# Attention and feed-forward on one core: another formula for the small part of the exponential, and one product for the linear path

## The chip, the cores and the metric

One of the eight cores of one Trainium2 chip runs the whole program. The metric is the time that the device needs for one execution, in microseconds; every time below is one of those or comes from one profiled execution. The engines are named as the profile names them: PE (TensorE's matmuls; PEld its weight loads), DVE (VectorE), ACT (ScalarE), POOL (GpSimd) and SP (SyncE, which here only issues DMAs).

## The reference

Shapes: `q` is 4 x 12288 x 128, `kv` 4 x 384 x 32 x 128, `w_sr` 128 x 128, `w_in` 128 x 2048, `w_out` 2048 x 128.

```python
kv_pool = kv.reshape(B, H // 4, 4, W // 4, 4, C).mean(axis=(2, 4))   # 768 keys per batch
k = v = kv_pool.reshape(B, -1, C) @ w_sr
s = (q @ k.transpose(0, 2, 1)) / np.sqrt(C)
a = np.exp(s - s.max(-1, keepdims=True))
x = (a / (a.sum(-1, keepdims=True) + 1e-09)) @ v                     # 49152 tokens x 128
h = x @ w_in
out = (h - np.tanh(h)) @ w_out
```

## The kernel before

The scores are small (the keys are taken about their mean), so exp(s) is split into 1 + s and a small rest exp(s)-1-s. The part 1 + s needs no scores at all: its product with the values is the 128 x 128 matrix M (the sum over keys of value times key) applied to q. Only the rest goes through the 768 keys. In the same way h - tanh(h) is taken about the batch's mean token: a first-order part, which is the 128 x 128 matrix A applied to the token's difference from the mean, and a third-order part, which needs the 2048 hidden values and is computed as h²(h+1) after a scaling.

Tokens are worked on in 96 groups of 512 (24 per batch). What one group needs, with the names and lines of the code:

- `rounded_q` (ACT, L1095) rounds q to the type that PE takes at its full rate (fp32r), and `lower_q` (POOL, L1148) keeps what the rounding lost.
- `scores` (PE, L1111): three tiles of 128 x 1024, each from two matmuls, in PSUM tiles called `big`, of which there are three. `exps` (ACT, L1115) takes exp, `beyond` (DVE, L1118) makes exp(s)-1-s in f16 (the tiles `r2`).
- The three `r2` tiles are summed in memory by DMAs: `copied` (SP) copies the first, `added` (POOL's queue, L1134) adds the second and the third. `shares` (PE, L1139) sums over the keys, and `share_left` (ACT, L1158) makes from it the factor t of every token.
- `straight` (PE, L1144) is M times q in three matmuls: upper part of M times rounded q, lower part of M times rounded q, upper part of M times the rest of q. `values` (PE, L1154) adds six matmuls of the values with `r2` into the same PSUM bank. `apart` (DVE, L1165) multiplies by t and gives df, the token's difference from the mean.
- `rounded` (POOL, L1168) rounds df to dr, and `lower_left` (POOL, L1194) keeps the rest, dl.
- The layer: `forth` (PE, L1225) makes eight `big` tiles of hidden values from dr. In seven of them `square` (ACT, L1229) and `cube` (DVE, L1232) make h²(h+1); in the eighth ACT copies (L1236) and POOL does one addition (L1239) and two products (L1243). `back` (PE, L1264) adds sixteen matmuls of the results into the bank `acc`, and another `straight` (PE, L1214) adds A times df, again in three matmuls. `result` (ACT, L1275) moves `acc` to SBUF and SP stores it.

That is 52 matmuls of 512 columns for each group. All of this overlaps: while a group's layer runs, the scores of groups two and three ahead are made. PSUM has eight banks: three `big` tiles of two banks, one bank `acc`, and one bank called `x`, which the sum over the shares, then the bank of `straight` and `values`, and the small products between batches use in turn.

The order is not written out by hand. Each operation is handed to a `Plan` with a label (`AT[...]` in eighths of a group's time, or an entry of the long list `PLACES`), an engine, a booked duration and the tiles it reads and writes. On each engine the operations of one lane are kept in the order of their labels; a label says which comes first on its own engine and is no time, so labels of two engines are not compared. Engines execute their queues in order, and so do the DMA queues of SP and POOL.

Before a batch starts, its keys are pooled by sixteen accumulating DMAs (L612, in POOL's queue, one per group), M and A are made, the scaled weights `winr` and `Wr` are made on POOL (L983, L1034), and the first-order terms are summed (L860 and L863 on DVE, L876 onwards on POOL, L1014 on POOL). Much of that runs beside the groups of the batch before. Ahead of the first group lie the loads of the weights and keys, and a conversion of the 64-bit words of the weights. At the end a verdict (`fits`) tests whether the approximations hold for the inputs; if they do not, a slow exact version runs afterwards.

Of the kernel before, what the change touches and what calls it, by code (L numbers as in the profile page):

```python
# [35 lines left out]
NEAR = 2.0**-12  # L36
# [7 lines left out]
LARGEST = 30000.0  # L44


class Plan:
# [3 lines left out]
    SOON = 0.1  # L51

# [46 lines left out]
    def run(self, between):  # L99
# [33 lines left out]
        while any(ready.values()):  # L133
            best = None
            for e, q in ready.items():
                if q:
                    starts = []
                    for r, i in q:
                        held = free.get("port", 0.0) if self.ops[i][5] else 0.0
# [13 lines left out]
            if port:  # L153
                free["port"] = now + us
# [35 lines left out]
    "within ym.i.3": -1236.8394829, "add win32 4": -1236.2365152, "first_stat stat": -1236.0688716,  # L190
# [14 lines left out]
    "apart df.3": -903.3427419, "rows norms 2": -903.3316533, "beyond r2.5.1": -903.3302341,  # L205
# [1381 lines left out]
```

## Time and profile before

| what | us |
|---|---|
| median of 3 runs (1278.62 to 1280.59) | 1279.99 |
| the profiled execution: span from the first to the last instruction | 1278.0 |
| PE busy (98% of the span), 5488 matmuls | 1252.7 |
| DVE busy (96%) | 1221.1 |
| ACT busy (93%) | 1188.8 |
| POOL busy (90%) | 1145.4 |

No separate time of the profiled execution is given; the median is 2.0 us above the span, which is what lies around it. Matmuls overlap in the pipeline and their ends are modelled, so PE's busy time says little: how long one holds PE is read from the starts of consecutive ones. The same holds in a smaller measure for the other engines, where an instruction begins before the shown end of the one ahead of it.

### The profile page before, as it was taken

The numbers are of one execution on the slowest core, as the hardware profiler recorded it, in microseconds if no ns is written. First come the engines' busy times: TensorE is split into PE (matmuls) and PEld (weight loads), VectorE is DVE, ScalarE is ACT, GpSimd is POOL, SyncE is SP. The second block draws the span as 40 slices with busy tenths as digits, with TensorE's granted clock in tenths as the row PEclk, the third lists the DMA queues.
The fourth block names the chain that finished last, engine by engine and source line by source line (L and its number), as shares of the span: only waits on it lengthen the run. The fifth ranks groups of instructions, "written<-read, shape, count | busy, mean of one in ns | idle before, by whom it ended". The sixth has DMA issues, their size and how long they took to land.

```text
span 1278.0 us, 17320 instructions
## 1 busy us (share of the span) xinstructions
PE 1252.7 (98%) x5488; PEld 880.8 (69%) x5488; DVE 1221.1 (96%) x1180; ACT 1188.8 (93%) x1416; POOL 1145.4 (90%) x981
## 2 busy tenths in 40 slices
PE   8999999999999999999999999999999999999997
PEld 7766676676767666676766767667667676766765
DVE  5999999999999999999999999999999999999996
ACT  4899999899999999999999999989999999999995
POOL 3799999899999997999999998999898988889886
PEclk9999999999999999999999999999999999999999
DMA  9276667347666653355666664344444444444431
GB/s 361 65 150 144 133 138 149 87 100 154 148 131 141 149 127 102 99 133 118 134 145 131 142 149 112 91 124 103 119 101 108 100 107 114 103 115 99 107 91 34
DMA packets 82947, 158.46 MB, mean 124 GB/s; under 512 B 9920, under 2 KB 12096, under 8 KB 82848
## 3 DMA queue, kind: packets, MB, share of 16 engines
q0 software_dynamic: 33552, 66.99, 31.7%
q1 hardware_dynamic: 49296, 90.29, 20.5%
q8 instruction: 45, 0.74, 0.3%
q14 instruction: 54, 0.44, 0.1%
HBM read 57.93 MB, written 25.39 MB: 65 GB/s over the span
## 4 chain that ended last, share of the span: by engine, by line
PE 70%; POOL 19%; issue 4%; DVE 3%; DMA 2%; ACT 2%; SPq 0%; POOLq 0%; DVEq 0%; ACTq 0%
PE big L1225 21%; PE acc L1264 20%; PE big L1111 9%; PE x L1154 7%; POOL rp L1243 5%; PE x L1144 4%; PE acc L1214 4%; POOL z L1243 4%; PE x L1139 3%; POOL rs L1134 3%; POOL ql L1148 2%; POOL z L1239 2%; POOL dr L1168 2%; DVE r L1118 1%; ACT E L1115 1%
## 5 line engine op out<-in xcount | busy, mean ns | idle before, releaser
L1232 DVE SCALAR_TENSOR_TENSOR r<-big,u 128x1024 fp32r<-128x1024 f32 x672 | 778.1, 1218 | 14.0 <-ACT u L1229 13.7
L1229 ACT ACTIVATE u<-big 128x1024 f32<-128x1024 f32 x672 | 661.8, 1033 | 35.0 <-PE big L1225 22.8
L1225 PE MATMUL big<-dr,winr 128*128 128x512 f32 x1536 | 510.1, 413 | 4.2 <-DVE r L1118 2.6
L1264 PE MATMUL acc<-r,Wr 128*128 128x512 f32 x1344 | 426.7, 410 | 0.6 <-DVE r L1232 0.6
L1118 DVE SCALAR_TENSOR_TENSOR r<-E,big 128x1024 f16<-128x1024 f32 x288 | 350.3, 1218 | 13.9 <-ACT E L1115 8.3
L1225 PEld LDWEIGHTS big<-dr,winr 128*128 128x128 f32 x1536 | 276.4, 188 | 101.0 <-DVE r L1118 26.1
L1115 ACT ACTIVATE E<-big 128x1024 f32<-128x1024 f32 x288 | 295.6, 1028 | 12.3 <-PE big L1111 2.3
L1264 PEld LDWEIGHTS acc<-r,Wr 128*128 128x128 f32 x1344 | 252.2, 188 | 64.6 <-DVE r L1232 1.5
L1243 POOL TENSOR_TENSOR rp<-z,v 128x1024 fp32r<-128x1024 f32 x96 | 258.9, 2697 | 0.2
L1243 POOL TENSOR_TENSOR z<-z,v 128x1024 f32<-128x1024 f32 x96 | 231.9, 2416 | 7.8
L1134 POOL DMA_DIRECT2D rs<-r x188 | 204.4, 1087 | 4.0 <-DMA rs<-r 2.3
L1111 PE MATMUL big<-qr,kTr 128*128 128x512 f32 x576 | 191.6, 414 | 0.4 <-ACT kTr L740 0.4
L1154 PE MATMUL x<-r,vvr 128*128 128x512 f16 x576 | 174.5, 385 | 0.0
L1194 POOL TENSOR_TENSOR dl<-df,dr 128x512 fp32r<-128x512 f32 x96 | 162.7, 1695 | 0.0
L1148 POOL TENSOR_TENSOR ql<-q,qr 128x512 fp32r<-128x512 f32 x96 | 161.4, 1681 | 0.5 <-ACT qr L1095 0.5
L1168 POOL TENSOR_SCALAR dr<-df 128x512 fp32r<-128x512 f32 x96 | 71.4, 744 | 76.0 <-DVE df L1165 72.1
L1111 PEld LDWEIGHTS big<-qr,kTr 128*128 128x128 f32 x576 | 101.3, 188 | 47.6 <-DVE r L1118 26.6
L1239 POOL TENSOR_SCALAR z<-v 128x1024 f32<-128x1024 f32 x96 | 111.4, 1161 | 0.5 <-ACT v L1236 0.5
L1236 ACT COPY v<-big 128x1024 f32<-128x1024 f32 x96 | 97.5, 1016 | 0.8 <-PE big L1225 0.6
L1154 PEld LDWEIGHTS <-vvr 128*128 128x128 f16 x576 | 33.5, 98 | 77.8 <-issue 77.5
L1264 PE MATMUL acc<-rp,Wr 128*128 128x512 f32 x192 | 77.0, 483 | 4.2 <-POOL rp L1243 4.0
L1275 ACT ACTIVATE o<-acc,At 128x512 f32<-128x512 f32 x96 | 65.8, 685 | 10.1 <-PE acc L1264 10.0
(182 smaller groups left out, 992.3 us busy)
## 6 DMA issues: line engine op xcount, KB each, us to landing
rs<-r POOLq DMA_DIRECT2D x188, 256.0 KB, 3.6
q<-in_q_dram SPq DMA_DIRECT2D x96, 256.0 KB
out_dram<-o SPq DMA_DIRECT2D x96, 256.0 KB
rs<-r SPq DMA_DIRECT2D x94, 256.0 KB
kvp<-in_kv_by_place_dram POOLq DMA_DIRECT2D x45, 384.0 KB, 5.2
winr<-in_kv_first_dram SPq DMA_DIRECT2D x8, 384.0 KB
kc<-inverse SPq DMA_DIRECT2D x12, 256.0 KB
r<-in_kv_by_key_dram SPq DMA_DIRECT2D x4, 512.0 KB
```

What stands on the lines that cost most here:

```text
L1111: PE.matmul(out=half(plan[s], h), lhsT=plan[kTr][:, n * P : (n + 1) * P], rhs=plan[qr], start=True, stop=True)
L1115: A.activation(out=plan[e], in_=plan[s], func=AF.Exp)
L1118: V.scalar_tensor_tensor(out=plan[r], in0=plan[e], scalar=-1.0, in1=plan[s], op0=ALU.add, op1=ALU.subtract)
L1134: PL.dma_start(out=plan[rs], in_=plan[r2s[k]], accum_op=ALU.add)
L1148: PL.tensor_tensor(out=plan[ql], in0=plan[qs], in1=plan[qr].bitcast(F32), op=ALU.subtract)
L1154: PE.matmul(out=plan[num], lhsT=plan[vvr][:, n], rhs=half(plan[f"r2.{g}.{k}"], h), start=(start and h == 0), stop=(stop and h == 1))
L1194: PL.tensor_tensor(out=plan[dl], in0=plan[df], in1=plan[dr].bitcast(F32), op=ALU.subtract)
L1225: PE.matmul(out=half(plan[hp], h), lhsT=plan[winr][:, f * P : (f + 1) * P], rhs=plan[dr], start=True, stop=True)
L1229: A.activation(out=plan[u], in_=plan[hp], func=AF.Square)
L1232: V.scalar_tensor_tensor(out=plan[r], in0=plan[hp], scalar=1.0, in1=plan[u], op0=ALU.add, op1=ALU.mult)
L1243: PL.tensor_tensor(out=plan[to], in0=plan[x], in1=plan[y], op=ALU.mult)
L1264: PE.matmul(out=plan[acc], lhsT=plan[Wr][:, 2 * n + h], rhs=half(plan[r], h), start=(start and h == 0), stop=(stop and h == 1))
```

## The change

- exp(s)-1-s becomes 4.5 ln(1-s/3)². ACT takes the logarithm of the score tile and writes w in f16 (128 x 1024); POOL multiplies w by itself (on DVE in the first three groups only). The factor 4.5 goes into the values and into t. DVE no longer reads the scores.
- All eight hidden tiles go through `square` on ACT and `cube` on DVE; the copy, the addition and the two products of the eighth are gone.
- The linear part of the attention passes to the output as one composed matrix B = M·A/K (K = 768): the layer's `straight` is now B upper times qr, B lower times qr, B upper times ql, and A times dl, where dl = df - M·q/K holds the small rest only. In the attention one matmul of M with rounded q stays, and a new DVE operation `keep` copies M·q/K out of the bank before `values` adds to it. B is made once per batch by a matmul (`through`), two ACT operations and a POOL subtraction.
- `share_left` moves from ACT to DVE. The nine products `first_times` of the later batches move from DVE to POOL.
- Buffers: six of `qr` and four of `ql` instead of five and two, six of `r` instead of four and two of `rp`, two of `rs` instead of three; the word tiles of the weights all use the three buffers `u` (one of each four had a tile of its own before).
- New labels in `AT` and a new list `PLACES`; the first five groups have no lanes; the verdict's early part starts fourteen groups before the end instead of twenty-four.

```diff
+            def roots(s=s, w=w):
+                A.activation(out=plan[w], in_=plan[s], func=AF.Ln, scale=-1.0 / 3, bias=1.0)
+            def beyond(w=w, r=r, k=k):
+                (V if k in on_v else PL).tensor_tensor(out=plan[r], in0=plan[w], in1=plan[w], op=ALU.mult)
-            def exps(s=s, e=e):
-                A.activation(out=plan[e], in_=plan[s], func=AF.Exp)
-            def beyond(s=s, e=e, r=r):
-                V.scalar_tensor_tensor(out=plan[r], in0=plan[e], scalar=-1.0, in1=plan[s],
-                                       op0=ALU.add, op1=ALU.subtract)
...
-        def straight(start, stop):
-            upper, lower = (plan[Mh][:, n] for n in range(2))
-            for n, (x, y) in enumerate(((upper, qr), (lower, qr), (upper, ql))):
-                PE.matmul(out=plan[num], lhsT=x, rhs=plan[y], start=(start and n == 0),
-                          stop=(stop and n == 2))
+        def straight():
+            PE.matmul(out=plan[num], lhsT=plan[Mh], rhs=plan[qr], start=True, stop=True)
+        def keep():
...
+                V.tensor_scalar(out=plan[kept], in0=plan[num], scalar1=1.0 / K, scalar2=None, op0=ALU.mult)
...
         def share_left():
...
+                V.tensor_scalar(out=plan[t], in0=plan[den], scalar1=-THIRD_OF / K**2, scalar2=1.0 / K,
+                                op0=ALU.mult, op1=ALU.add)
...
         def lower_left():
-            PL.tensor_tensor(out=plan[dl], in0=plan[df], in1=plan[dr].bitcast(F32), op=ALU.subtract)
+            PL.tensor_tensor(out=plan[dl], in0=plan[df], in1=plan[kept], op=ALU.subtract)
...
-            upper, lower = (plan[Ah][:, n] for n in range(2))
-            for n, (x, y) in enumerate(((upper, dr), (lower, dr), (upper, dl))):
+            upper, lower = (plan[Bh][:, n] for n in range(2))
+            for n, (x, y) in enumerate(((upper, qr), (lower, qr), (upper, ql), (plan[Ah], dl))):
...
-    ON_POOL = (0,)
...
-            V.tensor_tensor(out=plan[f"pr.{b}.{n}"], in0=winT[:, 4 * n : 4 * n + 4], in1=by, op=ALU.mult)
+            PL.tensor_tensor(out=plan[f"pr.{b}.{n}"], in0=winT[:, 4 * n : 4 * n + 4], in1=by, op=ALU.mult)
...
-    WORDS = {"i": ("u", "u", "u", "E"), "o": ("u", "u", "u", "z")}
+    WORDS = {"i": ("u", "u", "u", "u"), "o": ("u", "u", "u", "u")}
...
-        then=[6.19, 2.26, 3.01, 6.54, 1.52, 7.28, 8.03, 0.77],
-        back=[11.04, 6.93, 7.24, 7.85, 6.32, 8.76, 9.37, 5.71],
...
-        copied=-18.59, added=[-15.50, -11.66],
-        shares=-7.54, left=-6.81, straight=-6.02, apart=-2.72, rounded=-2.20, rounded_q=-24.34,
-        slope=4.93, result=11.47, lower_q=-12.50, lower_left=2.65, gather=-6.93)
+        rounded_q=-22.5, scores=[-24.19, -22.96, -21.97], roots=[-19.69, -19.48, -17.1],
+        beyond=[-17.77, -16.37, -16.06], copied=-18.97, added=[-15.26, -9.25], shares=-7.62,
+        left=-7.27, lower_q=2.48, straight=-6.63, keep=-5.82, values=[-4.43, -5.77, -5.74],
+        apart=-4.74, rounded=-1.06, lower_left=3.44,
+        forth=[-1.26, 0.4, 1.08, 1.64, 2.28, 4.6, 4.6, 4.93],
+        first=[2.36, 4.36, 5.05, 6.45, 7.24, 7.44, 8.85, 10.18],
+        then=[0.24, 1.97, 2.9, 3.19, 4.85, 5.21, 6.47, 7.21],
+        back=[4.13, 5.37, 6.96, 8.98, 5.8, 8.25, 9.57, 9.35], slope=4.85, result=14.11,
```

## Rows read from the trace of the kernel before

**Rows 1.** Output copies on ACT: count, shortest/median/longest, first and last start in us.

```profile
L1275 ACT ACTIVATE o<-acc,At x96: 673/686/693, 70.8 to 1271.3; 128x512 f32<-128x512 f32 x96
L1275 ACT ACTIVATE o<-acc,At x9: 677/686/688, 1143.9 to 1241.4; 128x512 f32<-128x512 f32 x9
```

**Rows 2.** PE in order of time: start, length, instruction; xN merges neighbours.

```profile
1110.11 0.63 PE L1225 MATMUL big<-dr,winr 128*128 128x512 f32 x2
1110.58 0.63 PE L1264 MATMUL acc<-r,Wr 128*128 128x512 f32 x2
1111.04 0.62 PE L1225 MATMUL big<-dr,winr 128*128 128x512 f32 x2
```

**Rows 3.** DVE in order of time, one group's work.

```profile
1111.83 8.07 DVE L1232 SCALAR_TENSOR_TENSOR r<-big,u 128x1024 fp32r<-128x1024 f32 x7
1119.82 2.50 DVE L1118 SCALAR_TENSOR_TENSOR r<-E,big 128x1024 f16<-128x1024 f32 x2
1122.24 0.68 DVE L1165 TENSOR_TENSOR df<-x,t 128x512 f32<-128x512 f32 x1
1122.93 1.22 DVE L1118 SCALAR_TENSOR_TENSOR r<-E,big 128x1024 f16<-128x1024 f32 x1
1124.07 1.23 DVE L1232 SCALAR_TENSOR_TENSOR r<-big,u 128x1024 fp32r<-128x1024 f32 x1
```

**Rows 4.** Stretches with a batch change: length, then busy us (instructions) of PE, PEld, DVE, ACT, POOL.

```profile
200.00:300.00 100.00, 96.33 (x429) 67.16 (x427) 98.04 (x99) 91.96 (x113) 91.94 (x90) 1.00 0.49 114
500.00:600.00 100.00, 97.46 (x432) 69.78 (x431) 94.34 (x92) 92.48 (x113) 96.60 (x86) 1.00 0.43 107
800.00:900.00 100.00, 97.18 (x424) 68.21 (x423) 94.76 (x93) 92.93 (x113) 96.00 (x94) 1.00 0.43 107
```

**Rows 5.** ACT in order of time, and its table load.

```profile
709.48 0.60 ACT L1158 ACTIVATE t<-x 128x512 f32<-128x512 f32 x1
709.95 1.96 ACT L1229 ACTIVATE u<-big 128x1024 f32<-128x1024 f32 x2
...
L515 ACT ACT_TABLE_LOAD x1 | 1.3, 1283 | 0.8 <-PEq L1545 0.8
```

**Rows 6.** POOL in order of time, one group's work; in brackets the idle time ahead.

```profile
1110.79 0.61 POOL L1168 TENSOR_SCALAR dr<-df 128x512 fp32r<-128x512 f32 x1 [1.51 <-DVE df L1165]
1111.38 1.04 POOL L1239 TENSOR_SCALAR z<-v 128x1024 f32<-128x1024 f32 x1
1112.50 2.42 POOL L1243 TENSOR_TENSOR z<-z,v 128x1024 f32<-128x1024 f32 x1
1114.87 0.86 POOL L1134 DMA_DIRECT2D rs<-r  x1
1115.51 2.67 POOL L1243 TENSOR_TENSOR rp<-z,v 128x1024 fp32r<-128x1024 f32 x1
1117.88 1.54 POOL L1194 TENSOR_TENSOR dl<-df,dr 128x512 fp32r<-128x512 f32 x1
...
1120.35 1.16 POOL L1134 DMA_DIRECT2D rs<-r  x1
```

**Rows 7.** POOL's work between batches by line: count, busy us, mean ns, idle before.

```profile
L612 POOL DMA_DIRECT2D kvp<-in_kv_by_place_dram x45 | 52.4, 1165 | 0.5 <-DMA kvp<-in_kv_by_place_dram 0.4
L983 POOL TENSOR_TENSOR winr<-win,kc 128x512 fp32r<-128x512 f32 x12 | 23.6, 1964 | 0.0
L1034 POOL TENSOR_TENSOR Wr<-wout,hb 128x512 fp32r<-128x512 f32 x16 | 20.3, 1395 | 1.0 <-DVE wout L535 0.7
L1014 POOL TENSOR_TENSOR Wg<-winT,hb 128x512 f32<-128x512 f32 x16 | 20.3, 1348 | 0.1
```

**Rows 8.** DMA issues: tensors, queue, count, KB each, median us to landing.

```profile
rs<-r POOLq DMA_DIRECT2D x188, 256.0 KB, 3.6
```

**Rows 9.** SP's queue in the first microseconds, in order of time.

```profile
3.30 0.44 SPq L497 DMA_DIRECT2D E<-in_moe_w_in_dram  x1
7.24 0.39 SPq L499 DMA_DIRECT2D u<-in_moe_w_out_dram  x1
```

More of the change, by code (lines that the diff above doesn't have):

```diff
@@ L34 @@
 ]
-NEAR = 2.0**-12
+NEAR = 0.000175
+THIRD_OF = 4.5
 SPREAD = 0.09
@@ L138, in run @@
                     for r, i in q:
-                        held = free.get("port", 0.0) if self.ops[i][5] else 0.0
+                        held = free.get("pool" if e == "DVE" else "port", 0.0) if self.ops[i][5] else 0.0
                         starts.append((max(free.get(e, 0.0), r, held), self.ops[i][0], i, r))
@@ L153, in run @@
             if port:
-                free["port"] = now + us
+                free["port" if e == "DVE" else "pool"] = now + us + (0.0 if e == "DVE" else self.HOLD)
             begun[i], done[i] = now, now + us + late
@@ L178 @@
 PLACES = {
[11 rows of a table removed]
-    "within ym.i.3": -1236.8394829, "add win32 4": -1236.2365152, "first_stat stat": -1236.0688716,
[14 rows of a table removed]
-    "apart df.3": -903.3427419, "rows norms 2": -903.3316533, "beyond r2.5.1": -903.3302341,
[10 rows of a table removed]
-    "copy winT 2": -609.7630918, "copy winT": -608.6881209, "lower rest.i.2": -604.1530543,
[3 rows of a table removed]
-    "fill ident": -586.1159995, "cut ident": -367.9673319, "exps e.2.2": -308.575726,
[60 rows of a table removed]
-    "load wsr": -163.4308876, "load planes.0": -160.2546256, "load_words words.i.3": -155.1177252,
[35 rows of a table removed]
-    "straight acc.2": 20.1579222, "rows norms": 21.113721, "square p4.0": 21.4626768,
[72 rows of a table removed]
[11 rows of a table added]
+    "cube r.0.1": -214.4454311, "load planes.0": -209.0608899, "load wsr": -207.6154104,
[67 rows of a table added]
+    "lower rest.o.0": 17.496, "copy winT 2": 17.4965, "rounded_q qr.2": 17.497, "rounded_q qr.3": 17.4975,
[5 rows of a table added]
+    "copy_moment Mn.0": 20.2845, "beside wg.0.1": 20.285, "copy winT": 20.286, "beside wg.0.0": 20.2865,
[27 rows of a table added]
+    "centre pc.1": 32.3785, "forth h.4.1": 32.5553818, "cube r.3.3": 32.6184438, "fill ident": 32.677,
[8 rows of a table added]
+    "first_slopes iv.0": 32.6935, "first_stat stat": 32.694, "scaled winr.0 3": 32.6945, "shift ym.o.3": 32.695,
+    "scaled winr.0 4": 32.6955, "scaled winr.0": 32.696, "scaled winr.0 2": 32.699, "share_left t.0": 32.6995,
+    "keep c.0": 32.7015, "apart df.0": 32.7025, "share_left t.1": 32.704, "keep c.1": 32.7055,
+    "apart df.1": 32.707, "share_left t.2": 32.7085, "keep c.2": 32.7095, "rows norms 2": 32.7155,
[39 rows of a table added]
+    "store_left left.1": 278.1005, "store_left left.2": 278.1015, "store": 278.102, "store_left left.3": 278.1025,
[48 rows of a table added]
+    "rows norms 5": 564.7956952, "through pb.3": 566.736489, "lower_through Bh.3": 568.1395,
[4 rows of a table added]
 }
@@ L911, in about_centre @@
                 pr = f"pr.{b}.{n}"
-                plan.op(first_at[n], "DVE", 0.65, partial(first_times, n), (f"cr.{b}", "winT"), (pr,), port=True)
+                plan.op(first_at[n], "POOL", 1.02, partial(first_times, n), (f"cr.{b}", "winT"), (pr,), port=True)
                 plan.op(first_at[n] + 0.1, "DVE", 0.62, partial(first_sums, n), (pr,), ((hb, n),))
@@ L1051, in upper_slopes, with through, upper_through, lower_through @@
             A.copy(out=plan[Am], in_=plan[pt][:, 0:P])
-            A.copy(out=plan[Ah][:, 0], in_=plan[Am])
-        def lower_slopes():
-            PL.tensor_tensor(out=plan[Ah][:, 1], in0=plan[Am], in1=plan[Ah][:, 0].bitcast(F32),
+            A.copy(out=plan[Ah], in_=plan[Am])
+        def through():
+            PE.matmul(out=plan[pb][:, 0:P], lhsT=plan[Mn], rhs=plan[Am], start=True, stop=True)
+        def upper_through():
+            A.activation(out=plan[Bm], in_=plan[pb][:, 0:P], func=AF.Copy, scale=1.0 / K)
+            A.copy(out=plan[Bh][:, 0], in_=plan[Bm])
+        def lower_through():
+            PL.tensor_tensor(out=plan[Bh][:, 1], in0=plan[Bm], in1=plan[Bh][:, 0].bitcast(F32),
                              op=ALU.subtract)
@@ L1094, in rounded_q @@
         def rounded_q():
-            A.copy(out=plan[qr], in_=plan[qs])
-        ago = math.floor(BUFS["q"] - (AT["lower_q"] - AT["added"][0]) / UN)
+            if ROUND_Q == "ACT":
+                A.copy(out=plan[qr], in_=plan[qs])
+            else:
+                PL.tensor_scalar(out=plan[qr], in0=plan[qs], scalar1=1.0, scalar2=1.0, op0=ALU.mult,
+                                 op1=ALU.mult)
+        ago = 3
         behind = () if g < ago + 3 else (f"first.{g - ago}",)
@@ L1149, in lower_q, with values @@
                              op=ALU.subtract)
-        def values(k, start, stop):
+        def values(k, stop):
             for h in range(2):
@@ new lines, in attention @@
+            if JOINED:
+                plan.op(s0 + AT["joined"], "POOL", 0.98, joined, (rs,), (rh,), late=0.33, lane=g >= LANED, port=True)
+        plan.op(s1 + AT["shares"], "PE", (0.235 if JOINED else 0.465) if g >= DIRECT else 1.36, shares,
+                ["ident"] + ([rh] if g >= DIRECT and JOINED else summed), (den,), late=PE_LATE[g >= SET], lane=g >= LANED)
+        plan.op(s1 + AT["left"], LEFT_BY, 0.48 if LEFT_BY == "ACT" else 0.61, share_left, (den,), (t,), late=SHORT[LEFT_BY][1][g >= SET], lane=g >= LANED)
@@ L1186, in attention @@
         terms.sort(key=lambda x: x[0])
+        plan.op(s1 + AT["straight"], "PE", 0.235, straight, (Mh, qr), (num,), late=PE_LATE[g >= SET], lane=g >= LANED)
+        plan.op(s1 + AT["keep"], KEPT_BY, SHORT[KEPT_BY][0], keep, (num,), (kept,), late=SHORT[KEPT_BY][1][g >= SET],
+                lane=g >= LANED)
         for n, (at, us, emit, of) in enumerate(terms):
[L1188 to L1189 removed]
@@ L1190, in attention @@
-        plan.op(s1 + AT["apart"], "DVE", 0.6 if g < SET else 0.63, apart, (num, t), (df,), late=DVE_LATE[g >= SET], lane=True)
-        plan.op(s1 + AT["rounded"], "POOL", 0.59, rounded, (df,), (dr,), late=POOL_LATE[g >= SET], lane=True)
+            plan.op(s1 + at, "PE", us, partial(emit, stop=(n == AN - 1)), of, (num,),
+                    late=PE_LATE[g >= SET] if g < SET or n == AN - 1 else 0.0, lane=g >= LANED)
+        plan.op(s1 + AT["apart"], "DVE", 0.6 if g < SET else 0.63, apart, (num, t), (df,), late=DVE_LATE[g >= SET], lane=g >= LANED)
@@ L1233, in cube @@
                                        op0=ALU.add, op1=ALU.mult)
[L1235 to L1260 removed]
+            plan.op(s0 + AT["forth"][n], "PE", PAIR[g >= SET], forth, (winr, dr), (hp,), late=PE_LATE[g >= SET], lane=g >= LANED)
+            first, then = s0 + AT["first"][n], s0 + AT["then"][n]
+            sb(u, "u", [P, WIDE], step=first)
+            plan.op(first, "ACT", 0.92, square, (hp,), (u,), late=ACT_LATE[g >= SET], lane=g >= LANED)
+            sb(r, "r", [P, WIDE], R32, step=then)
+            plan.op(then, "DVE", 1.137, cube, (hp, u), (r,), late=DVE_LATE[g >= SET], lane=g >= LANED)
             def back(start, stop, n=n, r=r):
@@ L1395, in fits @@
                 late=2.0, dma=1.0)
-        plan.op(step - 1, "DVE", 0.5, least, ("all_left",), ("most",))
+        plan.op(step - 1, "DVE", 0.9, least, ("all_left",), ("all_left", "most"))
         plan.op(step, "PE", 1.1, turn_left, ("most", "ident"), ("of_left",), late=0.2)
```

153 lines of the change are left out of this document (75 added, 78 removed), and 414 rows, old and new, of the table PLACES.

## The prediction

> **What bounds the kernel now.** I read the profile in this order. First the pace: the output copy of one group starts 12.72 us after that of the group before in the mean of the first 92 steps ((1241.4 - 70.8) / 92), and 12.2 us in undisturbed groups [rows 1, 3]. Then PE in order of time: the three pairs of matmuls start 0.465 us apart [rows 2], so one matmul holds PE for 0.2325 us and the 52 of a group for 12.09 us. Then DVE: seven cubes start between 1111.83 and 1119.82, 1.141 us each, and ten such operations and `apart` (0.69) make 12.10 us; the same cube comes again after 12.24 us [rows 3]. So PE and DVE are both full, and a plain group costs 0.14 us more than either needs. ACT and POOL have room: POOL stands idle for 1.51 us a group before `rounded` [rows 6].
>
> The mean step exceeds the plain one by 0.48 us, 45 us in 92 steps. Most of that is PE's own work for the next batch; PE's idle time in the three stretches with a change of batch is 3.67 + 2.54 + 2.82 = 9.0 us [rows 4].
>
> **PE.** Attention loses two matmuls of M, the layer gains one (four instead of three): 51 a group, 11.86 us. 96 x 0.2325 = 22.3 us go, if PE remains what sets the pace. `through` adds a small product in each later batch, priced like one matmul: 0.7 us in all.
>
> **DVE.** The three `beyond` leave, one cube and two short operations that read 512 columns from PSUM come. Those are not in the trace. Upper end: `apart`, which reads as much from PSUM with a second operand, 0.69. Lower end: half of a cube, 0.57 [rows 3]. I take 0.63: 8 x 1.141 + 0.69 + 2 x 0.63 = 11.08 us, 0.8 below PE. At either end it is below PE.
>
> **ACT.** ln replaces exp and a square the copy, tile for tile; I take each at the 0.93 us at which two squares follow each other, and `share_left` (0.47) leaves [rows 5]. ACT gets lighter. A logarithm dearer than exp costs nothing up to 0.2 us per tile: eleven tiles (10.2), two copies of 512 columns (0.47 each or a little more) are 11.2 us.
>
> **POOL.** What leaves occupies 1111.38 to 1114.87 and 1115.51 to 1117.88: 5.86 us. What stays is `rounded` 0.59, two DMA issues of 0.64 and the two subtractions in 1117.88 to 1120.35: 4.34 us [rows 6]. The three f16 products of 1024 columns are not in the trace. Upper end: the old product of as many f32 elements, 2.37 by the starts (2.7 by its shown length). Lower end: a subtraction that reads as many bytes, 1.23 [rows 6]. Whether bytes or elements set the pace no row says, so I take the middle, 1.8: 4.34 + 5.4 = 9.7 us. Between batches POOL also has 45 DMA issues (0.64), the scalings, and now nine `first_times` that I price like L1014 (1.35): 29 + 23.6 + three quarters of 40.6 + 12 = 95 us, or 1.27 in each of about 75 steps [rows 6, 7]. 11.0 is below 11.86, so the nine products are hidden too; without that cover they cost their 12 us.
>
> **Stalls.** Two amounts can come back: the 9.0 us of idle PE at the changes of batch [rows 4] and 0.14 us in each of 92 steps, 13 us [rows 2, 3]. DVE gets 0.8 us of room, and score tiles are free after ACT instead of after DVE; the eighth layer tile no longer passes through three POOL operations within its group. I take half of the first and a third of the second, 8.5 us; ends 0 and 22.
>
> **New hand-overs.** `values` now waits for `keep`, because it adds to the bank that `keep` reads. By the labels three pairs of matmuls (1.4 us) stand between; `keep` takes 0.63 us but may find one cube (1.14) ahead of it on DVE, so PE waits between 0 and about 0.4 us. Behind `values` in PE's queue stand `forth` and `back` of the layer, and ACT and DVE live on those. And the second `added` now stands directly ahead of `rounded` in POOL's queue, and on PE only four pairs (1.9 us) lie between the first use of dr and `shares`, which needs that DMA landed, 3.6 us after its issue [rows 8]. With `rounded` (0.6), what is missing, 1.1 us, is covered by POOL's wait in front of `rounded` as long as POOL is not full. I take 0.03 us a group, 3 us; ends 0 and 0.4 a group.
>
> **Start and end.** The fourth load of weight words, issued at 3.30, now waits for a `u` buffer as the fifth did until 7.24 [rows 9]: up to 4 us later, with the loads behind it in SP's queue. Against that, DVE saves about half of nine products there, up to 5 us. I take 0. The last three steps, without attention, took 29.9 us [rows 1]; with eight cubes as the longest load (8 x 1.141 = 9.1, with waits 9.4) they take 28.2: 1.7 less.
>
> **Sum.** 1278.0 - 22.3 + 0.7 - 8.5 + 3 - 1.7 = 1249.2 us of span, and with the 2.0 us by which the median stands above the span, 1251.
>
> **Rivals.**
> 1. Hand-overs eat the gain: a wait of 0.15 us a group at `values` or `shares` gives 96 x 0.15 - 3 = 11 us back, 1262. For it: one bank serves the shares, `straight`, `keep`, `values` and `apart` in turn, with DVE in it three times. Against: DVE has 0.8 us of room.
> 2. POOL becomes the bound: the slower side. Its place is the three products, queued in order with `rounded`. At the price of equal elements, 2.37, POOL needs 4.34 + 7.11 + 1.27 = 12.72 us in each of the 75 steps with work for a batch, where today's mean is (92 x 12.72 - 17 x 12.23) / 75 = 12.84. It decides from there: if `rounded` still waits 0.5 us for `apart` (today 1.51 [rows 6]) with the products queued behind it, a step takes 13.22, 28 us more in all; the other steps (11.95) and the end give 8 back: 1300. Below a sum of 7.2 us for products and wait it stays faster. The Trainium skill, GPSIMD Engine Reference, section "Elementwise — side-by-side cycle accounting", speaks for this rival: it holds a product of two inputs to about 2.6 cycles per element, because both operands come through one read port, and an estimate from it is 2.2 us whatever the type. The trace's 2.37 for f32 is near that; no row has f16.
> 3. The logarithm and the square need different tables, so ACT loads one at each change. Today one load of 1.28 us serves exp, square, copy and identity [rows 5]. Three logarithms among the squares make up to six loads a group: 96 x 6 x 1.28 = 740 us, about 1990. Nothing in the trace decides it, but the kernel's other ACT functions share one load. The Trainium skill, ScalarE: Activation LUTs, section "Table sets: the hidden batching unit", has exp and ln in one set and the cheap functions in every set; by that, the rival falls.
> 4. The change doesn't do what it says: the verdict fails and the exact version runs as well. The limit on the mean of the rest falls to 0.000175; computed from the reference's inputs, the largest is 0.000132. Chance below one per cent, a multiple of the time.
>
> **How the numbers follow.** My forecast 0.65, rival 1 0.13, rival 2 0.16 (0.03 of it still faster, at the element price with little wait, and 0.04 no change), rival 3 0.03, the rest (a slower start, rival 4) 0.03. 0.2% of the time, 2.6 us, is about what a measurement can tell from no change. Faster: 0.65 + 0.12 + 0.03 = 0.80; same 0.05; slower 0.15. The forecast's own range is 1241 (all stalls gone, short start) to 1260; 8 in 10 need the first rival and the near part of the second: 1240 to 1276.
>
> **What would show it.** Right: undisturbed groups every 11.9 to 12.0 us, matmul pairs still 0.465 us apart, DVE near 11.1 us a group with gaps, POOL's f16 products starting 1.6 to 2.0 us apart, one table load. Wrong: products 2.3 us or more apart and no idle time on POOL; PE idle before `values` on `keep` or before `shares` on the DMA in many groups; a second table load; a first output later than 75 us.

## The result: slower, and where the time went

The changed kernel takes 1290.62 us (median of 4 runs, 1288.35 to 1291.76), the kernel before 1280.14 beside it: ratio 1.0079 [1.0065, 1.0093], slower. The forecast was 1251, its range 1240 to 1276: wrong in sign and outside the range. The profiled execution's span is 1286.6 us against 1278.0.

First the pace again, as in [rows 1]: the output copies of the changed kernel, all of them, the first 25, and nine near the end; under them the first 25 of the kernel before.

```profile
L1305 ACT ACTIVATE o<-acc,At x96: 684/690/712, 85.8 to 1280.2; 128x512 f32<-128x512 f32 x96
L1305 ACT ACTIVATE o<-acc,At x25: 684/690/712, 85.8 to 398.5; 128x512 f32<-128x512 f32 x25
L1305 ACT ACTIVATE o<-acc,At x9: 684/690/691, 1152.2 to 1248.1; 128x512 f32<-128x512 f32 x9
```

```profile
L1275 ACT ACTIVATE o<-acc,At x25: 673/687/691, 70.8 to 381.3; 128x512 f32<-128x512 f32 x25
```

With [rows 1] these give the whole difference of the spans. The times before and after are differences of the starts above and of the spans:

| stretch | before | after | difference | forecast |
|---|---|---|---|---|
| to the first output | 70.8 | 85.8 | +15.0 | 0 |
| first to 25th output | 310.5 | 312.7 | +2.2 | -7.1 |
| 25th to 93rd output (68 steps) | 860.1 | 849.6 | -10.5 | -20.0 |
| last three steps | 29.9 | 32.1 | +2.2 | -1.7 |
| after the last output | 6.7 | 6.4 | -0.3 | 0 |

(The forecast's -22.3, +0.7, -8.5 and +3 make -27.1 for 92 steps; 68 of them are -20.0, 24 are -7.1.) So the change pays in the long middle, but only half of what was forecast, and loses 17 us up to the 25th output.

These 17 us are more than the start. At the ninth output the changed kernel is 27.4 us behind, and its first change of batch lies elsewhere: PE's first product with the second batch's keys comes at 125.18 instead of 234.85. Before and after:

```profile
L1275 ACT ACTIVATE o<-acc,At x9: 681/689/690, 70.8 to 169.7; 128x512 f32<-128x512 f32 x9
234.85 0.81 PE L668 MATMUL big<-kvp,wsr 128*128 128x384 f32 x2
```

```profile
L1305 ACT ACTIVATE o<-acc,At x9: 687/690/701, 85.8 to 197.1; 128x512 f32<-128x512 f32 x9
125.18 0.88 PE L683 MATMUL big<-kvp,wsr 128*128 128x384 f32 x2 [1.02 <-DMA kvp<-in_kv_by_place_dram]
```

The third, fourth and sixth step of the changed kernel take 16.9, 17.4 and 14.8 us (before: 12.2, 12.3 and 12.2); the kernel before pays for that change of batch in its steps 11 to 22, most in the 14th (19.8). Of the 17.2 us at the 25th output 15.0 are there at the first. Above 24 plain steps (12.24 and 12.13, next paragraph), the stretch with the first change of batch costs 16.7 us before and 21.6 after, 4.9 more, and the shorter plain step gives 2.7 back. In the 68 steps behind it the plain step gives 7.8 of the 10.5 us, and the two later changes of batch together some 2.7.

**The plain step.** Seven undisturbed steps, before and after: 85.7 / 7 = 12.24 and 84.9 / 7 = 12.13 us.

```profile
L1275 ACT ACTIVATE o<-acc,At x8: 677/686/687, 1143.9 to 1229.6; 128x512 f32<-128x512 f32 x8
```

```profile
L1305 ACT ACTIVATE o<-acc,At x8: 684/690/691, 1152.2 to 1237.1; 128x512 f32<-128x512 f32 x8
```

PE in order of time, as in [rows 2], DVE, as in [rows 3], ACT, as in [rows 5], and POOL, as in [rows 6], in one such step of the changed kernel:

```profile
1163.86 0.63 PE L1275 MATMUL big<-dr,winr 128*128 128x512 f32 x2
1164.33 0.62 PE L1138 MATMUL big<-qr,kTr 128*128 128x512 f32 x2
1164.78 1.04 PE L1192 MATMUL x<-r,vvr 128*128 128x512 f16 x4
1165.84 0.71 PE L1275 MATMUL big<-dr,winr 128*128 128x512 f32 x2
```

```profile
1163.72 0.68 DVE L1183 TENSOR_SCALAR c<-x 128x512 f32<-128x512 f32 x1
1164.47 1.22 DVE L1282 SCALAR_TENSOR_TENSOR r<-big,u 128x1024 fp32r<-128x1024 f32 x1
1165.95 1.22 DVE L1282 SCALAR_TENSOR_TENSOR r<-big,u 128x1024 fp32r<-128x1024 f32 x1 [0.26 <-ACT u L1279]
...
1167.78 5.94 DVE L1282 SCALAR_TENSOR_TENSOR r<-big,u 128x1024 fp32r<-128x1024 f32 x5
```

```profile
1165.79 1.05 ACT L1142 ACTIVATE w<-big 128x1024 f16<-128x1024 f32 x1
1166.69 1.06 ACT L1279 ACTIVATE u<-big 128x1024 f32<-128x1024 f32 x1
1167.96 1.03 ACT L1279 ACTIVATE u<-big 128x1024 f32<-128x1024 f32 x1 [0.21 <-PE big L1275]
```

```profile
1167.88 0.61 POOL L1213 TENSOR_SCALAR dr<-df 128x512 fp32r<-128x512 f32 x1 [1.42 <-DVE df L1207]
1168.46 3.74 POOL L1145 TENSOR_TENSOR r<-w 128x1024 f16<-128x1024 f16 x2
```

The reader is to see: pairs of f32 matmuls still start 0.465 us apart (1163.86, 1164.33); two of POOL's f16 products take 3.74 us, 1.87 each, and POOL still waits 1.42 us before dr; `keep` (c<-x) shows 0.68 us, as `apart` does. Those prices were right. But no engine is without gaps: the four f16 matmuls from 1164.78 take 0.9 us, and the next layer product starts only at 1165.84, 0.15 us after the shown end of DVE's cube that began at 1164.47 and whose PSUM tile it takes. Three of the waits of the run, line by line (engine, what for: us, times, longest), before and after:

```profile
DVE r L1232 <- ACT u L1229: 13.7, 25, 1.8
ACT u L1229 <- PE big L1225: 22.8, 39, 1.3
```

```profile
DVE r L1282 <- ACT u L1279: 75.8, 198, 1.5
ACT u L1279 <- PE big L1275: 75.2, 199, 2.5
POOL kvp L627 <- DMA kvp<-in_kv_by_place_dram: 15.7, 11, 3.7
```

DVE waits for ACT five times as long as before, ACT for PE three times as long. All score and layer tiles pass through three PSUM tiles, the layer's from PE to ACT to DVE and back to PE, the scores' from PE to ACT and back; my reading is that DVE, which had been a full engine (it had 0.14 us left of 12.24 [rows 3]), now takes part in a ring of waits in which each engine is late by what the one before it was late. The experiments below bear on that.

**The start.** PE in order of time, before and after, up to the first score:

```profile
30.90 0.95 PE L850 MATMUL acc<-col,win 128*128 128x1 f32 x8
...
33.28 0.72 PE L1111 MATMUL big<-qr,kTr 128*128 128x512 f32 x2 [0.43 <-ACT kTr L740]
```

```profile
32.32 1.86 PE L863 MATMUL acc<-col,win 128*128 128x1 f32 x8 [1.29 <-DVE col L744]
...
44.61 0.94 PE L1138 MATMUL big<-qr,kTr 128*128 128x512 f32 x2
```

The first score starts at 44.61 instead of 33.28. Eight products of one column take 1.86 us instead of 0.95: the granted clock is 0.50 there (1.2 GHz, the lower of its two levels, 1.2 and 2.4), after a stretch in which PE was busy for 1.41 of 4 us. Stretches of the changed kernel; length, busy us (instructions) of PE, PEld, DVE, ACT, POOL, then the clock:

```profile
28.00:32.00 4.00, 1.41 (x5) 0.49 (x4) 2.12 (x3) 1.55 (x4) 2.53 (x2) 0.93 1.07 387
...
36.00:40.00 4.00, 4.00 (x20) 4.00 (x20) 1.03 (x2) 2.46 (x4) 0.00 (x0) 0.50 0.34 98
```

POOL issues the loads that gather the second batch's keys from 43.36 on (before: from 65.27), and eleven of the run's 45 wait for the one ahead of them (15.7 us, above; before 0.4 [rows 7]); and DVE's f16 product takes 0.68 us alone, but three of them 3.61 beside GpSimd's scaling:

```profile
53.81 3.61 DVE L1145 TENSOR_TENSOR r<-w 128x1024 f16<-128x1024 f16 x3
...
57.95 0.68 DVE L1145 TENSOR_TENSOR r<-w 128x1024 f16<-128x1024 f16 x1
```

```profile
54.92 1.34 POOL L1027 TENSOR_TENSOR Wg<-winT,hb 128x512 f32<-128x512 f32 x1
59.94 0.88 POOL L627 DMA_DIRECT2D kvp<-in_kv_by_place_dram  x1 [3.68 <-DMA kvp<-in_kv_by_place_dram]
```

The word loads that the prediction named come later than it assumed. The fourth, issued at 3.30 before, and the first of the second weight, at 7.24 [rows 9], are issued here at:

```profile
13.33 0.33 SPq L512 DMA_DIRECT2D u<-in_moe_w_in_dram  x1
18.11 0.39 SPq L514 DMA_DIRECT2D u<-in_moe_w_out_dram  x1
```

That is 10 and 11 us later, where the prediction had up to 4. No run varied these loads, so what they cost is open.

### The profile page after: what moved, and what is told of

Same layout as the page of the kernel before. It is cut to its first block, busy times and chain, and to the rows that moved or that the text cites. A ratio compares the mean times of both kernels' runs of the same rounds, so it can differ in the third digit from the quotient of the medians.

```text
span 1286.6 us, 17480 instructions
## 1 busy us (share of the span) xinstructions
PE 1247.9 (97%) x5400; PEld 875.9 (68%) x5400; DVE 1148.2 (89%) x1181; ACT 1151.0 (89%) x1329; POOL 1116.4 (87%) x977
## 4 chain that ended last, share of the span: by engine, by line
PE 76%; POOL 10%; DMA 6%; DVE 4%; issue 2%; ACT 1%; SPq 0%; DVEq 0%; POOLq 0%; ACTq 0%
PE big L1275 25%; PE acc L1294 22%; PE x L1192 9%; PE big L1138 8%; PE acc L1264 5%; POOL r L1145 4%; DMA rs<-r 3%; PE x L1174 3%; DVE r L1282 3%; PE x L1177 1%; DMA kvp<-in_kv_by_place_dram 1%; POOL rs L1166 1%; POOL ql L1186 1%; POOL dl L1245 1%; ACT u L1279 1%
## 5 line engine op out<-in xcount | busy, mean ns | idle before, releaser
L1282 DVE SCALAR_TENSOR_TENSOR r<-big,u 128x1024 fp32r<-128x1024 f32 x768 | 921.1, 1221 | 84.2 <-ACT u L1279 75.8
L1279 ACT ACTIVATE u<-big 128x1024 f32<-128x1024 f32 x768 | 778.8, 1032 | 80.8 <-PE big L1275 75.2
L1145 POOL TENSOR_TENSOR r<-w 128x1024 f16<-128x1024 f16 x279 | 596.0, 2229 | 0.0
L1294 PE MATMUL acc<-r,Wr 128*128 128x512 f32 x1536 | 482.6, 406 | 0.2
L1142 ACT ACTIVATE w<-big 128x1024 f16<-128x1024 f32 x288 | 296.2, 1031 | 11.1 <-PE big L1138 9.0
L1245 POOL TENSOR_TENSOR dl<-df,c 128x512 fp32r<-128x512 f32 x96 | 169.2, 1762 | 0.0
L1138 PEld LDWEIGHTS big<-qr,kTr 128*128 128x128 f32 x576 | 102.2, 188 | 36.2 <-ACT u L1279 12.2
L1200 DVE TENSOR_SCALAR t<-x 128x512 f32<-128x512 f32 x96 | 65.4, 681 | 7.3 <-PE x L1174 7.2
L1207 DVE TENSOR_TENSOR df<-x,t 128x512 f32<-128x512 f32 x96 | 65.4, 681 | 4.3 <-POOL dl L1245 1.8
L627 POOL DMA_DIRECT2D kvp<-in_kv_by_place_dram x45 | 52.2, 1159 | 18.9 <-DMA kvp<-in_kv_by_place_dram 15.7
L1183 DVE TENSOR_SCALAR c<-x 128x512 f32<-128x512 f32 x96 | 65.3, 680 | 0.6 <-PE x L1177 0.6
L1174 PE MATMUL x<-rs,share 128*128 128x512 f16 x188 | 56.8, 384 | 8.6 <-DMA rs<-r 7.6
```

The costliest lines, as they stand in the source:

```text
L1138: PE.matmul(out=half(plan[s], h), lhsT=plan[kTr][:, n * P : (n + 1) * P], rhs=plan[qr], start=True, stop=True)
L1142: A.activation(out=plan[w], in_=plan[s], func=AF.Ln, scale=-1.0 / 3, bias=1.0)
L1145: (V if k in on_v else PL).tensor_tensor(out=plan[r], in0=plan[w], in1=plan[w], op=ALU.mult)
L1174: PE.matmul(out=plan[den], lhsT=share, rhs=x, start=(n == 0), stop=(n == len(of) - 1))
L1245: PL.tensor_tensor(out=plan[dl], in0=plan[df], in1=plan[kept], op=ALU.subtract)
L1279: A.activation(out=plan[u], in_=plan[hp], func=AF.Square)
```

## Experiments

Ratios are to the kernel before, timed on the same chip in the same job; the changed kernel stands at 1.0079. "Step" is the plain step, "25th" the start of the 25th output copy (398.5 in the changed kernel). Edits are shown shortened (`r` for `plan[r]`). First and 25th outputs come from one profiled execution each. The first run below (two matmuls a group fewer) keeps the start's order and shows 84.4 and 396.6 instead of 85.8 and 398.5, so differences of one or two us there carry no weight.

### What sets the plain step

**Two matmuls fewer.**

```
- ((upper, qr), (lower, qr), (upper, ql), (plan[Ah], dl))
+ ((upper, qr), (plan[Ah], dl))
```

> The changed kernel, with two of the four matmuls of the layer's straight left out (B lower times qr and B upper times ql), so 49 matmuls a group instead of 51. Theory A, the ring: an undisturbed group takes 12.12 us because the three PSUM tiles called big go round PE, ACT and DVE with no room in the dense part of the group, and PE is not what sets the pace. Then a group stays at 12.1 us and the time within about 6 us of the changed kernel's 1290.6. Theory B, PE: 51 matmuls and what PE loses between them set the pace. Then 0.465 us a group go, 96 x 0.465 = 45 us: about 1246, and a group of 11.66 us.

1287.31 us, 1.0058 [1.0036, 1.0080]. Step 12.13: 4% of PE's work is gone, and the step did not move. PE is not the bound of the changed kernel's plain step.

**No `keep`.**

```
- plan.op(s1 + AT["keep"], ..., keep, (num,), (kept,), ...)
- PL.tensor_tensor(out=dl, in0=df, in1=kept, op=subtract)
+ PL.tensor_tensor(out=dl, in0=df, in1=df, op=subtract)
```

> The changed kernel without the operation keep (the rest dl is made from df alone, so the linear part is not taken out of it): 0.68 us less on DVE in each group, and values no longer wait for DVE. Theory A, the ring: ACT, not keep, is what the third cube waits for, so a group stays near 12.1 us and the time within 6 us of 1290.6. Theory C, the new hand-over: the wait at keep is the 0.26 us a group by which 12.12 exceeds the 11.86 us of 51 matmuls; then 91 x 0.26 = 24 us go: about 1267.

1276.56 us, 0.9970 [0.9960, 0.9981], between the two. The step falls by 0.03 only, to 12.09; from the 25th to the 93rd output it is 841.3 instead of 849.6, so 6 of these 8 us are in the changes of batch; 4.9 us come up to the 25th output. `keep` does not make PE wait in every group, as forecast, but it costs where DVE has a batch's work as well.

**Squares of 512 columns.**

```
- A.activation(out=u, in_=hp, func=Square)
+ A.activation(out=half(u, 0), in_=half(hp, 0), func=Square)   # the cube reads this half twice
```

> The changed kernel, with ACT's square reading and writing only 512 of its 1024 columns (DVE's cube uses them twice, so it does the same amount of work): ACT gets 0.43 us lighter in each of eight tiles. Theory A, the ring: the round trip of a PSUM tile gets shorter, PE becomes the pace, and a group falls from 12.12 to about 11.9 us: 20 us less, about 1270. Theory B, PE: a group stays at 12.12 us, the time at 1288 to 1291.

1263.12 us, 0.9875 [0.9847, 0.9904]: more than either expected. The step falls to 11.75. The squares' mean goes from 1032 to 596 ns, 3.5 us of ACT a group, and the step follows by 0.37. It may have met PE there, which then shows 48.00 of 48 us (below): 43 matmuls at 0.2325 us and eight f16 ones at 0.22 to 0.23 (the values and the shares) are some 11.8 us.

**Both.** 

> Two of the four products of the layer's straight part left out and the squares on 512 of 1024 columns, both in one kernel (each was run alone). If the 11.75 us of a plain step with short squares is PE's floor (51 x 0.2304), the step falls to 11.3 to 11.45 (49 x 0.2304 = 11.29), some 35 us less, 1222 to 1232. If it is another loop through the three tiles, the step stays at 11.7 to 11.76 and the time at 1258 to 1264.

1261.08 us, 0.9838 [0.9821, 0.9855], near the second reading. The step is 11.68 (81.8 / 7), not 11.3: with 49 matmuls another limit comes after 0.07 us. The rows of the five kernels, 1100 to 1148 us, in the order changed, two matmuls fewer, no `keep`, short squares, both; columns as above:

```profile
1100.00:1148.00 48.00, 47.94 (x210) 33.99 (x209) 44.66 (x46) 45.12 (x51) 41.13 (x40) 1.00 0.44 108
```

```profile
1100.00:1148.00 48.00, 46.71 (x202) 32.27 (x201) 45.09 (x46) 45.12 (x51) 41.13 (x40) 1.00 0.42 105
```

```profile
1100.00:1148.00 48.00, 48.00 (x207) 33.65 (x206) 42.16 (x41) 45.81 (x52) 41.84 (x45) 1.00 0.42 106
```

```profile
1100.00:1148.00 48.00, 48.00 (x213) 35.44 (x212) 45.19 (x47) 34.43 (x52) 44.90 (x46) 1.00 0.45 111
```

```profile
1100.00:1148.00 48.00, 47.56 (x206) 33.57 (x204) 45.56 (x47) 35.17 (x54) 45.32 (x47) 1.00 0.44 110
```

A busy share does not name the bound: PE shows 47.94 of 48 in the changed kernel (its ends are modelled) while two of its matmuls can go for nothing. Neither PE's nor DVE's own work is the bound: taking 0.47 us from PE or 0.68 from DVE changes the step by 0.03 at most. ACT's squares are on what sets it, but ACT is not full either, for it waits 75.2 us for PE's tiles; POOL, which waits 1.42 us a step before dr, was not varied. That points to a loop of hand-overs through the three tiles. The trace offers one: ACT works without a gap from the square at 1161.52 (1173.64 less one step) to the end of the one at 1166.69, 6.2 us; its cube on DVE can start after `apart`, at 1167.78, and the second cube after it is done at 1171.2; the score that needs that tile starts at 1171.54; four pairs on PE, 1.9 us, lead to the square at 1173.64. That these links add up to the step proves nothing, as every chain from one instruction to the same one a step later does. It would have to be tight at each link, and at 1171.54 it is not seen to be: the pair ahead of that score started at 1171.08, so PE came free just then. Which loop sets the step was not shown.

**Another order.**

```
- DVE_LATE = (0.2, 0.1);  lower_q=2.48; apart=-4.74; then=[0.24, 1.97, 2.9, 3.19, ...]
+ DVE_LATE = (0.2, 0.28); lower_q=5.81; apart=-4.4;  then=[0.59, 0.93, 2.49, 2.68, ...]
...
```

> The same instructions in another order in every group: the hand-over after a VectorE operation is booked at 0.28 us instead of 0.1, and the places within the cycle are moved (the second product and the remains of q later, apart and the third cube a little). Theory A, the step hangs on loops through the three tiles that an order can shorten only a little: plain step 12.05 to 12.12, changes of batch some 3 us shorter in all, 1283 to 1289. Rival B, the order of the cycle is what costs the 0.26 us: step 11.9 to 12.0, 1272 to 1280.

1296.60 us, 1.0115 [1.0088, 1.0142]: slower than both expected. The step is 12.14, so this other order does not give the 0.26 us back (one order tried does not speak for all); the changes of batch became 6 us dearer, not 3 cheaper.

**VectorE's nine products back.**

```
- PL.tensor_tensor(out=pr, in0=winT[...], in1=by, op=mult)
+ V.tensor_tensor(out=pr, in0=winT[...], in1=by, op=mult)
```

> Takes back one part of the change: the nine first_times products between batches run on VectorE again (0.65 us each) instead of GpSimd (1.0 to 1.4). Theory A, VectorE is on the path at the changes of batch, as the run without `keep` says: 3 to 6 us slower, 1293 to 1297. Rival B, GpSimd is full there: 3 to 9 us faster, 1282 to 1288. Plain steps 12.12 us under both.

1295.87 us, 1.0112 [1.0096, 1.0129], as theory A said: 5 us lost. From the 25th to the 93rd output it takes 854.2 us instead of 849.6. This part of the change is worth keeping, and DVE is on the path at the changes of batch.

### What holds the start

**A held clock.**

```
+ if b == 0:
+     busy(8)
...
+ if n == 7:
+     busy(14)
...
+ def busy(count):
+     for _ in range(count):
+         PE.matmul(out=plan["ph.0.0"][:, G - P : G], lhsT=ident, rhs=ident, start=True, stop=True)
...
+ if n == 1:
+     busy(12)
```

> The changed kernel, with 34 small extra matmuls ahead of the first group, in three places where PE waits between 28 and 44 us, so that the granted clock stays at its upper level (it fell to half from about 31 to 45 us). Theory A, the clock: the half clock lies on the way to the first output; holding it brings the first output from 85.8 us to about 81 and the time down by about 5 us. Theory B, the order: those matmuls wait for ACT and DVE anyway, and the late first output comes from the order of the loads and conversions alone; the clock returns 0 to 1 us.

1288.27 us, 1.0063 [1.0040, 1.0087]. The clock reads 1.00 in the start; the first output comes at 87.7, 1.9 later, the 25th at 397.2, 1.3 earlier. But the added products hold PE's queue too:

```profile
32.85 2.84 PE L729 MATMUL acc<-ident 128*128 128x128 f32 x24
35.53 0.95 PE L873 MATMUL acc<-col,win 128*128 128x1 f32 x8
```

The products of one column start at 35.53 instead of 32.32, 3.2 us later, and from there to the first score it takes 10.0 us instead of 12.3 (45.49 and 44.61 are the first scores). So the held clock gave back at least 2.3 us on that way, and the added products took more than that ahead of it. Together they move the time little; what the half clock alone costs was not shown.

**A quarter of the weights' own product.**

```
- for f in range(h * FT // 4, (h + 1) * FT // 4):
+ for f in range(FT // 4 if h == 0 else 0):
```

> Leaves out 24 of the 32 products of the product of the weights with themselves (its norm is then wrong), which in the changed kernel run from 47.09 to 54.5 us, ahead of the first group's `shares`, on the bank that `shares` needs; the order is kept. Theory A, the start is late because these products and the half clock hold PE and that bank: first output at 82 us or before (85.8), 1283 to 1287 us. Rival B, the start is held by the words, the keys and the products of the first groups elsewhere: first output at 85 to 86.5, 1289 to 1291.

1287.12 us, 1.0051 [1.0034, 1.0068]. First output 84.6, 25th 395.1: 3.4 us in all, less than theory A wanted at the first output, more than B. The first score already starts at 43.19 instead of 44.61, ahead of the products left out, so the 1.2 us at the first output are not theirs, and the rest is little above what single executions differ by. The medians are 3.5 us apart, and the single times overlap (1284.6 to 1289.19 against 1288.35 to 1291.76).

**The first group early.** The places of the start are given anew, many of them earlier, among them:

```
+ PLACES.update({"turn turned.0": -274.0, "product 0 WW": -271.5, "small_keys kTr.0": -269.0,
+     "scores s.0.0": -268.0, "roots w.0.0": -267.5, "beyond r2.0.0": -267.0, "shares den.0": -261.0,
+     "apart df.0": -258.5, ...})
```

> Only the order of the start is changed: the second half of the weight transposes, the product of the weights with themselves, the first keys and the first group's scores, logarithms, products, shares and values are placed as early as in the kernel before (first score near 34 us instead of 44.6). Theory A, the first output is late because the first group's attention starts late: first output at 78 us or earlier (85.8), 1278 to 1285 us. Rival B, the start is full of work that must be done by then, the next groups' attention and GpSimd's scalings above all, and an earlier first group only pushes the following ones: the first layer tile no more than 6 us earlier, the first output at 80 or later, the sixth output not earlier, 1290 to 1300 us.

1298.22 us, 1.0138 [1.0118, 1.0158]: rival B. PE and POOL of that run in order of time:

```profile
36.63 1.73 PE L1713 MATMUL big<-qr,kTr 128*128 128x512 f32 x5 [0.45 <-ACT kTr L1326]
...
59.15 2.09 PE L1609 MATMUL acc<-Wg,wout 128*128 128x129 f32 x8 [2.58 <-POOL Wg L1602]
...
63.60 2.10 PE L1749 MATMUL x<-r,share 128*128 128x512 f16 x6
...
65.57 0.71 PE L1850 MATMUL big<-dr,winr 128*128 128x512 f32 x2
```

```profile
54.20 0.99 POOL L1788 TENSOR_SCALAR dr<-df 128x512 fp32r<-128x512 f32 x1 [0.17 <-DVE df L1782]
```

The first score comes 8 us earlier, dr is ready at 55.2 instead of 67.0, and yet the first layer product starts at 65.57 instead of 67.05: it stands in PE's queue behind slopes that wait 2.58 us for a scaling on GpSimd, and behind the shares of the next group. The third and fourth step take 22.6 and 23.7 us, and the 25th output comes at 407.1, 8.6 later. The late first score, which I had read as the cause, is not it alone. And in this run the granted clock fell a second time, after a stretch in which PE was busy for 0.57 of 3 us: eight slopes take 2.09 us there instead of 1.05. Columns as above:

```profile
56.00:59.00 3.00, 0.57 (x2) 0.13 (x2) 3.00 (x3) 2.62 (x4) 3.00 (x3) 0.84 0.42 80
59.00:62.00 3.00, 2.85 (x11) 2.67 (x12) 2.31 (x2) 0.00 (x0) 3.00 (x4) 0.50 0.01 3
```

**A plain form of the nine early products**, alone and with the first group early.

```
- V.tensor_tensor(out=r, in0=w, in1=w, op=mult)
+ V.scalar_tensor_tensor(out=r, in0=w, scalar=1.0, in1=w, op0=mult, op1=mult)
```

> The nine f16 products that VectorE makes for the first three groups (0.68 us alone, up to 2.30 beside a product on GpSimd) are written as scalar_tensor_tensor, about 1.14 us if it costs what a cube costs; the order is kept. Theory A, the waits of the two engines for each other (2.7 us on VectorE, some 0.3 us each on four of GpSimd's operations) are on the path of the start: none of the nine is longer than 1.3 us, GpSimd's Wg beside them is back at 1.04, first output 1.5 to 3 us earlier than 85.8. Rival B, they are covered or the dearer form eats the gain: first output within 1 us, the time within 2 us of 1290.6.

> The run with the first group's attention early, with the same plain form of the nine products. There PE waits 2.58 us for Wg and 10 us pass between dr and the first layer product. Theory A, the two engines' waits for each other stretch GpSimd's scalings: first layer product at 63 us or earlier (65.6), first output at 82.5 or earlier (85.0), 1294 to 1296 us. Rival B, it is the order of PE's queue and the half clock there: first layer product at 65 to 66, 1297 to 1300 us.

1293.40 us, 1.0096 [1.0077, 1.0116], and 1299.91, 1.0152 [1.0130, 1.0173]. Neither helps. The premise was wrong: the new form waits just as well. DVE of the second run:

```profile
55.40 1.99 DVE L1721 SCALAR_TENSOR_TENSOR r<-w 128x1024 f16<-128x1024 f16 x1 [0.59 <-ACT w L1717]
```

That is 1.99 us where 1.22 is usual (two others there take 2.06 and 2.29). So these two runs do not price the waits. (The profiled execution of the first had its loads 4 us late, first output 92.9, so its trace decides nothing.)

**No gathering of the second batch.**

```
+ if w and b == 1:
+     return
  PL.dma_start(out=kvp, in_=kv_by_place[b - 1, w], accum_op=add)
```

> Leaves out 15 of the 16 accumulating loads by which GpSimd gathers the second batch's keys (its keys are then wrong); the order of all else is kept. In the changed kernel they are issued from 43.4 to 120 us, each waiting in GpSimd's queue for the one before (3.68 and 3.24 us at 59.9 and 65.1), in the kernel before from 65.3 on and with next to no wait. Theory A, these waits hold the scalings, dr and the accumulations behind them and so the start: first output at 82 us or earlier (85.8), fourth and fifth step shorter by 2 us or more, 1276 to 1284 us. Rival B, the start is held elsewhere: first output within 1.2 us, 1286 to 1291.

> The same left out of the run with the first group's attention early. Theory A: with both waits gone the first layer product comes at 62 us or earlier (65.6), the first output at 80 or earlier (85.0), 1280 to 1288 us. Rival B, PE waits there for the scaled weights and not for what stands behind the loads: first output at 84 to 85.5, the steps after it as long as before, 1293 to 1299.

1283.45 us, 1.0023 [1.0013, 1.0034], and 1291.98, 1.0083 [1.0065, 1.0100], so 7.2 and 6.2 us less than the same orders with the loads. Output copies of the first:

```profile
L1307 ACT ACTIVATE o<-acc,At x25: 683/688/707, 82.9 to 392.1; 128x512 f32<-128x512 f32 x25
```

2.9 us of it are there at the first output (theory A wanted 3.8, B 1.2 at most), 6.4 at the 25th. Of the 2.9, 0.8 lie ahead of the loads left out: the first score starts at 43.83 instead of 44.61. The third and fourth step are 1.2 and 0.9 us shorter. So the loads, their waits and their 0.9 us of issue each hold about a third of the 17.2 us lost by the 25th output. They are not all that makes those steps long, which still take 15.7 and 16.5 us.

With the first group early too, the first output comes at 82.7 instead of 85.0, and the third and fourth step take 19.8 and 22.5 us instead of 22.6 and 23.7: neither theory. The first layer product comes at 63.31 instead of 65.57, but the loads' waits are not why: PE waits 2.55 us for Wg as before, and then the clock is up, so eight slopes take 1.16 us and not 2.09. From the first of them to the layer product PE does the same instructions in 3.7 us, and took 6.4 at half clock. PE of that run, and a stretch of it as above:

```profile
59.63 1.16 PE L1611 MATMUL acc<-Wg,wout 128*128 128x129 f32 x8 [2.55 <-POOL Wg L1604]
59.00:62.00 3.00, 2.37 (x19) 2.27 (x20) 2.81 (x2) 0.84 (x2) 3.00 (x3) 1.00 0.01 3
```

So this pair of runs does not price the loads at the first layer product; it shows what the half clock costs, 2.7 us, where PE has work that counts.

## Why the prediction was wrong

- **"22.3 us go, if PE remains what sets the pace": failed.** The price was right, the condition was not. The step fell by 0.11, not 0.23 us, and two matmuls less change nothing (12.13): PE no longer sets the pace. I read PE (12.09) and DVE (12.10) as full engines and the 0.14 above them as slack that comes back. With less work on PE and DVE, something else sets the step at 12.13; that it is hand-overs between the engines through the three tiles fits the runs, and which of them was not shown.
- **"8.5 us of stalls come back": failed in the steps.** The two later changes of batch did become some 2.7 us shorter, near the 3 that two thirds of 4.5 would be; the 4 us from the plain steps did not come. I gave DVE 0.8 us of room in the mean of a step. The room is not where the cubes need it: ACT runs seven operations and DVE five cubes without a gap, and in the rest of the step both wait (75.2 and 75.8 us in the run).
- **"Hand-overs +3": wrong place.** No wait of PE for `keep` or for the DMA in every group: PE waits 1.1 us in all at `values`. Without `keep` the time is some 14 us less, nearly all of it in the start and at changes of batch.
- **Start "I take 0": failed by 15.0 us**, and by 17 at the 25th output. I listed a word load that waits for a buffer, at up to 4 us (it came 10 later), and looked no further. The diff moved nearly every place of the start and brought the gathering of the second batch 22 us forward, its first product on PE 110 us; I had the rows of the loads' issues and did not lay them beside the first outputs.
- **Tail -1.7: failed by 3.9** (32.1 us instead of 29.9). Not pursued.
- **Right:** 0.2325 us a matmul; POOL's f16 product 1.87 against 1.8, and below the 2.2 that the prediction had as an estimate beside it, so rival 2 fell: POOL has 1.42 us left before dr. `keep` and `left` 0.68 shown against `apart`'s 0.68, the upper end. ln as dear as the square (1.03).
- **Rival 3 fell, by a load more than expected.** ACT's table loads in the changed kernel, us and ns:

```profile
L1118 ACT ACT_TABLE_LOAD x1 | 1.3, 1283 | 0.8 <-PEq L1576 0.8
L1142 ACT ACT_TABLE_LOAD x1 | 1.3, 1283 | 0.0
```

One at the beginning, one at the first logarithm (47.24), none after it, so logarithm, square and copy share a set here. The prediction had this from the Trainium skill, ScalarE: Activation LUTs, section "Table sets: the hidden batching unit" (cheap functions, the copy among them, are in every set). The trace agrees; that the square is one of them the page does not say, only the trace shows it. The second load stands in the start, ahead of the first group.

Rival 1 named the right kind of thing, waits that eat the gain, at the wrong place and with the wrong size.

Of the 17 us up to the 25th output, start and first change of batch together, the runs settle one part, the gathering loads (up to 6.4), and bound another loosely, the weights' own product (3.4 at most). The half clock was not priced by itself. Most of the 17 us stays open, with the order of PE's queue, the word loads that come 10 us later, the second batch's work so early and the two engines' waits for each other as suspects that were not separated. No kernel that leaves nothing out beat the kernel before.

## What to carry to other kernels

Before a gain is booked on the full engine, look at the others that hand the same tiles round (here PE, ACT, DVE and back to PE): where several of them lie close to the step, as PE and DVE did at 12.1 of 12.24 us, work taken from one need not come back in full. A busy share of 97% does not make an engine the bound; leaving out a little of its work and looking at the step does. And a change that moves loads in a start is priced from those loads: who issues them, what waits behind them, and which outputs stand after. Where the reading is a first output of one execution, look at the granted clock and at the instructions ahead of the edit before calling the difference an effect.

## Hardware seen on the way

DVE's f16 product of 1024 columns, both inputs in SBUF, took 0.68 us alone and 2.30 with GpSimd's two-input product (1.34 instead of 1.04) beside it; written as scalar_tensor_tensor it took 1.22 alone and 1.99 to 2.29 beside GpSimd's work. The cubes, which read one of their inputs from PSUM, keep 1.22 beside GpSimd's products. The Trainium skill, SBUF — State Buffer, section "Who interferes with whom", has the rule: a DVE instruction with two SBUF inputs and a GpSimd instruction that reads SBUF exclude each other, and the later one waits for the other to end. The rows agree in the main: both engines' products grew, and the DVE product of 2.30 us (54.51 to 56.81) ended 0.55 us after GpSimd's (56.26); which of the two held the other first they do not tell. By that rule the plain form could not have helped, and `beyond`, which before read the scores from PSUM, did not have the trouble. f16 matmuls started 0.22 to 0.23 us apart, a little closer than the f32 ones (0.2325): with short squares a step with all 51 takes 11.75.
